# Attention and mixer on one core: q and k of the last three batches turned by transposing transfers instead of TensorE

## The chip, the cores and the metric

The kernel runs on one core of one Trainium2 chip. The metric is the device time of one execution in microseconds; the median of three runs is given. One more execution was taken with the hardware profiler, and its times are those of the views below.

## What is computed

The reference has two parts, one behind the other. The first is a causal attention with a selective bias, for 8 batches of 8 heads with 576 positions of 64 numbers:

```
scores = q @ k^T / 8
cum    = cumsum(max(s, 0))
scores = scores + min(-(cum_i - cum_j), 0), -1e9 above the diagonal
x      = softmax(scores) @ v           # heads side by side: 8 x 576 x 512
```

The second mixes along the sequence by a rank of 32 and then along the channels:

```
u   = x + (x^T U V)^T
out = u + max(u @ w_ch1, 0) @ w_ch2    # 512 -> 2048 -> 512
```

Inputs and output are float32; the kernel works in bf16 with sums in float32.

## The kernel before, in words

**Pairs.** Two heads make a pair, so that there are 32 pairs, n = 0 to 31, four in a batch. The score matmuls (`scores`, L391) need q and k with the 64 numbers of a head on the partitions and the positions along the free axis. Such an operand lies in a slot: 128 partitions x (2 heads) x (576 of q, 576 of k, and a zeroed end). Partitions 64 to 67 hold four rows, pieces of the cumulated s and ones, which add the bias inside the same matmul. From pair 8 on three slots are used in turn (`slot_of`).

**Loads.** GpSimd (POOL) issues the loads of q and k from HBM, float32 turned to bf16 on the way: one transfer for q and one for k of a whole batch, 576 KB each (`load_qk`, L113 for the later batches, L118 for the first). 72 rows lie on the partitions, with 8 runs of 64 numbers for each head. There are two buffers each for q and k, so that the load of batch b waits until the transposes of batch b-2 are over. v goes into one of two slots, by five transfers per batch (L169).

**Turning.** `transposes(n)` turns a pair on TensorE (PE): for each of the two heads four 72x128 blocks of q and four of k, each block a matmul with an identity (L303), into one PSUM tile per head. Two copies per head (64x576, L323) bring it from PSUM into the slot; most are on VectorE (DVE), a few on ScalarE (ACT), by a list in `copies`. Before them the SP queue issues two transfers (L289) that bring the four rows of the pair from a scratch tensor in HBM, `rows_hbm`, which was written once at the start (L222).

**Scores and values.** `scores(n)` makes the scores of a pair in four steps; ACT takes the exponential of each (L409, L421, L427) into pT, and VectorE masks the diagonal blocks (L335). `values(n)` multiplies with v (L455); VectorE makes a reciprocal of the sum (L464) and the quotient x_sb (L465). SP then issues a transposing transfer of x_sb into xT (L472), which the mixing along the sequence (`seqmix`, with uT written at L509) adds later.

**Channel mixing as fill.** `chanmix` makes the hidden layer (L624, evacuated by ACT at L1001) and the output by a scheme with seven products of quarters (L682, sums on VectorE at L660 and L696, stores by SP at L706). It is a generator, and `step_fill` takes one step of it between the steps of attention, so that PE always has work that waits for nothing. At its fourth step a transposing transfer by SP makes u_sd from uT (L988, 128x2048). The PSUM tiles of fill, transposes, values and mixing come in turn from one pool of four buffers (`pwork`).

**Order.** The main loop from L1204 goes over n. In iteration n it makes `transposes(n+1)` with the fill between, then `scores(n)`, then mixing if it is due, then `values(n-1)`. The order on PE and POOL is that of the program. VectorE, ACT and SP also work strictly in order, but for the part after the first batch their order is chosen by a scheduler when the kernel is built.

Of the kernel before, what the change touches and what calls it, by code (L numbers as in the profile page):

```python
# [13 lines left out]
BF16 = mybir.dt.bfloat16  # L14
# [25 lines left out]
def kernel(  # L40
# [12 lines left out]
    nc = tc.nc  # L53
    traced = len(nc.cur_bb.bb.instructions)
    E = mybir.EngineType
    B, H, S, D = q.shape
# [6 lines left out]
    BH = B * H  # L63
    NP = BH // 2
    PB = NP // B
    TP, TT = 72, 8
    NG = B * S // 512
    KA = D + 4
    NF = FF // 128
    FT = 2  # L70

    consts = ctx.enter_context(tc.tile_pool(name="consts", bufs=1))
    loads = ctx.enter_context(tc.tile_pool(name="loads", bufs=2))
# [17 lines left out]
    rows = s_early[:BH, : 8 * S].rearrange("p (r c s) -> p r c s", r=4, c=2)  # L91
# [9 lines left out]
    q_t, k_t = {}, {}  # L101

    def alloc_qk(b):
        q_t[b] = loads.tile([TP, H, TT * D], BF16, tag="q_sd", name="q_sd")
        k_t[b] = loads.tile([TP, H, TT * D], BF16, tag="k_sd", name="k_sd")

    def in_runs(b, h):
        return b > 2 or b == 2 and h >= 4

    def load_qk(b, h, n):  # L110
        for dst, src in ((q_t[b], q), (k_t[b], k)):
# [71 lines left out]
    def slot_of(n):  # L183
        return slots[n % NSLOT if n < 2 * PB else (n + 1) % 3]
# [32 lines left out]
                in_=rows[2 * n + hh : 2 * n + hh + 1].rearrange("n r c s -> n r (c s)"),  # L217
            )

    rows_hbm = nc.dram_tensor("rows_hbm", (4, BH, S), BF16, kind="Internal").ap()  # L220
    for r, n_r, c in ((0, 3, 1), (3, 1, 0)):
        nc.sync.dma_start(  # L222
            out=rows_hbm[ds(r, n_r), ds(2 * PB, BH - 2 * PB)].rearrange("r n s -> n r s"),
            in_=rows[2 * PB :, ds(r, n_r), c, :],
        )

    w1_sb = consts.tile([128, 4, FF], BF16)
    w2_sb = consts.tile([128, NF, DM], BF16)
# [55 lines left out]
    def transposes(n):  # L284
        b, hp = divmod(n, PB)
        slot = slot_of(n)
        if b > 0:
            for r, n_r, c in ((0, 3, 1), (3, 1, 0)):
                nc.sync.dma_start(  # L289
                    out=slot[ds(D + r, n_r), :, ds(c * S, S)],  # L290
                    in_=rows_hbm[ds(r, n_r), ds(2 * n, 2)],
                )
        tps = {}

        def turn(hh, c):
            if c == 0:
                tile = pwork()
                tps[hh] = tile.bitcast(BF16)[:, : 2 * 4 * TP].rearrange(
                    "p (c t m) -> p c t m", c=2, t=4
                )  # L300
            src = (q_t[b], k_t[b])[c]
            for t2 in range(4):
                nc.tensor.transpose(  # L303
                    tps[hh][:, c, t2, :],
                    src[:, 2 * hp + hh, ds(t2 * 128, 128)],
                    identity[:TP, :TP],
                )

        if b == 0:
            for hh in range(2):  # L310
                turn(hh, 0)
            yield
        for hh in range(2):
            if b > 0:
                turn(hh, 0)
            turn(hh, 1)
            tp = tps[hh]
            dst = slot[0:D, hh, 0 : 2 * S]
            for par in range(2):
                src = tp[par * D : par * D + D]  # L320
                if in_runs(b, 2 * hp):
                    by_run = dst.rearrange("p (c t two m) -> p c t two m", c=2, t=4, two=2)
                    copies(n, hh, par)(by_run[:, :, :, par, :], src)  # L323
                else:
                    in_turn = dst.rearrange("p (c m t two) -> p c m t two", c=2, t=4, two=2)
                    copies(n, hh, par)(  # L326
                        in_turn[:, :, :, :, par], src.rearrange("p c t m -> p c m t")
                    )
            yield

    def mask(dst, n_tiles, w, on_pool=False):
        if on_pool:
# [146 lines left out]
    def seqmix(b):  # L479
        x_sb = x_of.pop(b)  # L480
        up = pwork()[:, 0:128]
        for dt in range(4):
            for t in range(5):
                nc.tensor.matmul(
                    up[:, ds(dt * R, R)],
                    lhsT=x_sb[:, dt, t, :],
                    rhs=U_sb[:, t, 0:R],
                    start=(t == 0),
                    stop=(t == 4),
                    skip_group_check=True,  # L490
                )
        uxT = work.tile([128, 128], BF16, tag="uxT", name="uxT")
        nc.vector.tensor_copy(uxT, up)
        yield

        up = pwork()[:, 0:128]
        nc.tensor.matmul(up, lhsT=uxT, rhs=identity, start=True, stop=True)
        ux = work.tile([128, 128], BF16, tag="ux", name="ux")
        nc.vector.tensor_copy(ux, up)
        yield  # L500
        xT = xT_of.pop(b, None)
        cut = 512 - 64 * b

        def evac(dt, lo, hi, src):

            g, at = (b, 64 * b + lo) if lo < cut else (b + 1, lo - cut)
            dst = uT(g)[:, dt, at : at + hi - lo]
            if xT is not None:
                nc.vector.tensor_tensor(dst, src, xT[:, dt, lo:hi], op=ALU.add)  # L509
            elif dt == 2:  # L510
                nc.scalar.copy(dst, src)
            else:
                nc.vector.tensor_copy(dst, src)

        pair = pscore()
        banks = [pair[:, 0:512], pair[:, 512:1024], pwork(), pwork()]
        if xT is None:
            for dt in range(4):
                for t in range(4):
                    nc.tensor.matmul(  # L520
                        banks[dt][:, ds(t * 128, 128)],
                        lhsT=x_sb[:, dt, t, :],
                        rhs=identity,
                        start=(t == 0),
                        stop=False,
                        skip_group_check=True,
                    )
        for dt in range(4):
            nc.tensor.matmul(
                banks[dt],  # L530
                lhsT=ux[ds(dt * R, R), :],
                rhs=V_sb[ds(dt * R, R), 0:512],
                start=(xT is not None),
                stop=True,
                skip_group_check=True,
            )
        pair = pair.rearrange("p (a b) -> p a b", a=2)
        for dt, src in ((slice(0, 2), pair), (2, banks[2]), (3, banks[3])):
            for lo, hi in ((0, cut), (cut, 512)):
                if lo < hi:  # L540
                    evac(dt, lo, hi, src[..., lo:hi])
            yield
        ut = pwork()[:, 0:256].rearrange("p (a b) -> p a b", a=4)
        for dt in range(4):
            if xT is None:
                nc.tensor.matmul(
                    ut[:, dt, :],
                    lhsT=x_sb[:, dt, 4, :],
                    rhs=identity[:, :64],
                    start=True,  # L550
                    stop=False,
                    skip_group_check=True,
                )
            nc.tensor.matmul(
                ut[:, dt, :],
                lhsT=ux,
                rhs=V_end[:, dt, :],
                start=(xT is not None),
                stop=True,
                skip_group_check=True,  # L560
            )
        evac(slice(0, 4), 512, S, ut)
        yield
# [597 lines left out]
    def load(b):  # L1161
        alloc_qk(b)
        for h in range(0, H, 4 if b == 2 else H):
            load_qk(b, h, 4 if b == 2 else H)
# [38 lines left out]
    pace[1] = 11  # L1203
    for n in range(2 * PB, NP + 2):  # L1204
        b, hp = divmod(n, PB)
        if hp == 0 and b < B - 1:
            load(b + 1)
        mixing = seqmix(b - 1) if hp == 1 and b > FT else iter(())
        if b == B:
            fill_with(3)  # L1210
            for _ in range(3):
                step(mixing)
                fill_with(2)
        if n > 2 * PB and n + 1 < NP:
            for at, _ in enumerate(transposes(n + 1)):
                step_fill()
                if at == 0:
                    step(mixing)
        if 2 * PB + 1 < n < NP:
            for at, _ in enumerate(scores(n, pT_of(n))):  # L1220
                step_fill()
                if at == 1:
                    step(mixing)
        for _ in mixing:
            fill_with(1)
        if hp == 1 and FT < b < B:
            fill.append(chanmix(b - 1))
            pace[1] = 12 if b < 6 else 10
        if 2 * PB < n <= NP:
            run(values(n - 1, pT_of(n - 1)))  # L1230
        if hp == 0 and 2 <= b < B - 1:
            load_v(b + 1)
# [70 lines left out]
```

## Time and profile before

| | |
|---|---|
| median of 3 runs | 361.6 us (361.57 to 361.84) |
| the profiled execution | 362.13 us |
| its span, first to last instruction | 360.4 us |
| granted TensorE clock, mean | 0.999 |
| ScalarE busy, VectorE busy | 212.8 us, 274.5 us |
| pairs 20 to 31, transposes on PE | from 161.2 to 262.7 us |
| loads of q of batches 5, 6, 7 issued at | 118.08, 154.91, 192.45 us |
| x_sb into xT, time in SP's queue | 1.2 to 2.1 us, x24 |
| u_sd, time in SP's queue | 1.94 to 8.11 us, x6 |

A timeline has a line for a stretch of equal instructions: start, time, engine, source line, output and inputs, and how many; brackets at the end give the idle time before it and who released it. Durations of matmuls overlap, since they are pipelined; what one costs is seen from the start of the next. "SPq" is the queue of SP: the time that it took to issue a transfer, not the transfer itself. Times of day are microseconds from the start of the span.

### The profile page before, as it was taken

The page shows a single profiled execution, that of the slowest core. Times are in us where ns is not written, and L with a number is a line of the kernel's source. Part 1 is how long each engine was busy: PE and PEld are TensorE (multiplying, and loading weights), DVE is VectorE, ACT ScalarE, POOL GpSimd, SP SyncE. Part 2 cuts the span into 40 slices and gives each one's busy share as a digit, 9 for nine tenths or more (in the row PEclk, how much of TensorE's full clock was granted, in tenths as well). Part 3 has the DMA queues.
Part 4 walks back from the last instruction along what each step waited for, and adds up shares of the span by engine and source line. Part 5 has one row for each costly group of instructions (what it writes and reads, how often), then busy time and mean ns, then how long its engine had stood idle before and what let it go on. Part 6 is the DMA issues. An engine that isn't in the chain of part 4 may idle for free.

```text
span 360.4 us, 9583 instructions
## 1 busy us (share of the span) xinstructions
PE 349.2 (97%) x3987; PEld 256.5 (71%) x4026; DVE 274.5 (76%) x608; ACT 212.8 (59%) x322; POOL 84.1 (23%) x102
## 2 busy tenths in 40 slices
PE   8999999999999999999999999999899999999996
PEld 3685656666598667876688667876488548888885
DVE  8685776688789758985699569985797769676774
ACT  4786966747761677257833786358743554675710
POOL 8897363514040404040304022000000000000000
PEclk9999999999999999999999999999999999999999
DMA  7999999999999999989994999162032515010022
GB/s 101 155 200 196 175 181 102 155 135 136 109 103 106 141 121 81 85 113 123 122 97 66 135 142 85 51 149 58 0 49 67 136 33 116 29 60 31 30 89 87
DMA packets 156163, 37.41 MB, mean 104 GB/s; under 512 B 140760, under 2 KB 154488, under 8 KB 156120
## 3 DMA queue, kind: packets, MB, share of 16 engines
q0 software_dynamic: 113136, 18.50, 90.2%
q1 hardware_dynamic: 42696, 18.11, 29.2%
q8 instruction: 31, 0.51, 0.7%
q10 hardware_dynamic: 288, 0.20, 0.2%
q14 instruction: 12, 0.10, 0.1%
HBM read 37.25 MB, written 9.70 MB: 130 GB/s over the span
## 4 chain that ended last, share of the span: by engine, by line
PE 78%; DVE 8%; ACT 4%; issue 3%; POOL 3%; DMA 2%; DVEq 0%; ACTq 0%; POOLq 0%
PE pwork L624 22%; PE pwork L682 13%; PE quarter L682 10%; PE pscore L391 9%; PE pwork L455 7%; PE parts L912 6%; PE pwork L303 3%; PE pwork L643 3%; DVE uT L509 3%; DMA v_slot<-in_v_dram 2%; ACT pT L409 2%; ACT hT L1001 2%; DVE slot L660 1%; PE pwork L912 1%; PE pscore L624 1%
## 5 line engine op out<-in xcount | busy, mean ns | idle before, releaser
L624 PE MATMUL pwork<-uT,w_sb 128*128 128x512 bf16 x401 | 105.9, 379 | 2.6 <-ACT hT L1001 0.9
L1001 ACT ACTIVATE hT<-pwork 128x512 bf16<-128x512 f32 x108 | 65.2, 608 | 38.4 <-PE pwork L624 38.2
L409 ACT ACTIVATE pT<-pscore 128x1024 bf16<-128x1024 f32 x56 | 56.4, 1030 | 49.0 <-PE pscore L391 48.2
L624 PEld LDWEIGHTS <-w_sb 128*128 128x128 bf16 x448 | 38.3, 98 | 35.9 <-issue 1.3
L391 PE MATMUL pscore<-slot 68*128 68x320 bf16 (+1 forms) x500 | 55.4, 246 | 0.5 <-ACT pT L409 0.2
L391 PEld LDWEIGHTS <-slot 68*128 68x128 bf16 x564 | 41.3, 97 | 16.6 <-issue 1.0
L169 POOL DMA_DIRECT2D v_slot<-in_v_dram x40 | 33.8, 862 | 80.3 <-PE pwork L455 67.7
L682 PEld LDWEIGHTS <-hT 128*128 128x128 bf16 x496 | 46.3, 98 | 7.1 <-DVE uT L509 0.5
L335 DVE TENSOR_TENSOR pT<-pT,keep 128x512 bf16<-128x512 bf16 (+1 forms) x81 | 28.7, 354 | 21.7 <-ACT pT L409 15.9
L323 DVE COPY slot<-pwork 64x576 bf16<-64x576 bf16 x76 | 34.4, 453 | 4.6 <-PE pwork L303 3.7
L455 PEld LDWEIGHTS <-pT 128*128 128x128 bf16 x870 | 32.6, 98 | 7.1 <-issue 1.2
L455 PE MATMUL pwork<-v_slot,pT 128*128 128x65 bf16 x870 | 36.1, 194 | 1.1 <-DVE slot L326 0.6
L465 DVE TENSOR_TENSOR x_sb<-pwork,rec 128x320 bf16<-128x320 f32 x64 | 31.2, 489 | 1.4
L421 ACT ACTIVATE pT<-pscore 128x1024 bf16<-128x1024 f32 x29 | 30.3, 1044 | 2.6 <-PE pscore L391 2.4
L682 PE MATMUL pwork<-w_sb,hT 128*128 128x256 bf16 x240 | 30.6, 273 | 0.0
L326 DVE COPY slot<-pwork 64x576 bf16<-64x576 bf16 x30 | 24.1, 803 | 6.9 <-PE pwork L303 6.5
L682 PEld LDWEIGHTS <-slot 128*128 128x128 bf16 x256 | 24.1, 98 | 4.6 <-issue 1.6
L113 POOL DMA_DIRECT2D q_sd<-in_q_dram x6 | 12.6, 2107 | 44.1 <-PE pwork L303 33.5
L464 DVE RECIPROCAL rec<-pwork 128x5 f32<-128x5 f32 x64 | 12.1, 190 | 13.2 <-PE pwork L455 12.8
L682 PE MATMUL pwork<-w_sum,slot 128*128 128x256 bf16 x160 | 20.3, 272 | 0.7 <-DVE o_sb L696 0.7
L303 PEld LDWEIGHTS <-q_sd 72*128 72x128 bf16 x256 | 14.6, 98 | 8.7 <-DMA q_sd<-in_q_dram 1.1
L303 PE MATMUL pwork<-identity,q_sd 72*128 72x72 bf16 x256 | 18.0, 196 | 0.4 <-DMA q_sd<-in_q_dram 0.4
(164 smaller groups left out, 537.8 us busy)
## 6 DMA issues: line engine op xcount, KB each, us to landing
out_dram<-o_sb SPq DMA_DIRECT2D x34, 256.0 KB
v_slot<-in_v_dram POOLq DMA_DIRECT2D x32, 128.0 KB, 7.2
w_sb<-in_moe_w_ch_dram POOLq DMA_DIRECT2D x4, 1024.0 KB, 13.1
q_sd<-in_q_dram POOLq DMA_DIRECT2D x5, 576.0 KB, 15.1
k_sd<-in_k_dram POOLq DMA_DIRECT2D x5, 576.0 KB, 20.7
q_sd<-in_q_dram POOLq DMA_DIRECT2D x4, 288.0 KB, 13.3
k_sd<-in_k_dram POOLq DMA_DIRECT2D x4, 288.0 KB, 12.1
q_sd<-in_q_dram POOLq DMA_DIRECT2D x4, 144.0 KB, 5.2
```

Source lines behind the costliest of these rows:

```text
L169: nc.gpsimd.dma_start(out=vt[:rows_t, t, :, 0:D], in_=v[b, :, ds(t * 128, rows_t), :].rearrange("h p d -> p h d"),)
L303: nc.tensor.transpose(tps[hh][:, c, t2, :], src[:, 2 * hp + hh, ds(t2 * 128, 128)], identity[:TP, :TP],)
L323: copies(n, hh, par)(by_run[:, :, :, par, :], src)
L335: nc.vector.tensor_tensor(dst, dst, keep[:, :, 0:w].to_broadcast([128, n_tiles, w]), op=ALU.min)
L391: nc.tensor.matmul(dst, lhsT=slot[0:KA, hh, ds(S + j * 128, 128)], rhs=slot[0:KA, hh, lo:hi], start=True, stop=True,)
L409: nc.scalar.activation(pT[:, hh, 0:1024], near, EXP, scale=scale)
L421: nc.scalar.activation(pT[:, :, 1024:1536], mid.rearrange("p (a b) -> p a b", a=2), EXP, scale=scale)
L455: nc.tensor.matmul(po[:, i, :], lhsT=pT[:, hh, ds(place(j, i), 128)], rhs=vt[:, j, h, :], start=(j == 0), stop=(j == i), skip_group_check= ...
L465: nc.vector.tensor_tensor(x_sb[:, hp, :, ds(hh * D, D)], po[:, :, 0:D], rec.to_broadcast([128, 5, D]), op=ALU.mult,)
L624: nc.tensor.matmul(f1, lhsT=w1_sb[:, kt, ds(nf * 128, 128)], rhs=u[:, kt, :], start=(kt == 0), stop=(kt == 3),)
L682: nc.tensor.matmul(acc[:, i, :], lhsT=a[:, kt, ds(i * 128, 128)], rhs=b[:, kt, :], start=(begin and i == 0 and kt == 0), stop=(kt == HF - ...
L1001: nc.scalar.activation(hT[:, nf, :], f1, RELU)
```

## The change

For batches 5, 6 and 7 (`ZB = 5`, pairs 20 to 31) q and k are not turned by PE any more.

- The load puts 96 rows on the partitions, six runs per head, and the two heads of a pair side by side. So it is one transfer per head for q and one for k, sixteen per batch of 144 KB each. They stand in the program at the last pair of batch b-2 rather than at the first of b-1.
- `turn_pair(n+2)`, at the head of iteration n, issues two transposing transfers on SP, one for q and one for k: 96x768 becomes six blocks of 128x96. Head 0 lands on partitions 0 to 63 of the slot, head 1 on 64 to 127, both in the first half of the slot.
- `part_pair(n+1)`, in the place of `transposes(n+1)`, has one VectorE copy, 64x1152, that brings head 1 to partitions 0 to 63 of the second half, and then one transfer of the four rows. These rows lie on partitions 64 to 67, where head 1 lay, so that the transfer waits for the copy.
- The rows of these batches come from a second scratch tensor, `full_hbm`, with the ones already in it, by one transfer instead of two.

```diff
-        q_t[b] = loads.tile([TP, H, TT * D], BF16, tag="q_sd", name="q_sd")
-        k_t[b] = loads.tile([TP, H, TT * D], BF16, tag="k_sd", name="k_sd")
+        rows = TP if b < ZB else TR          # TR, RT = 96, 6
+        q_t[b] = loads.tile([rows, H, TT * D], BF16, tag="q_sd", name="q_sd")
+        k_t[b] = loads.tile([rows, H, TT * D], BF16, tag="k_sd", name="k_sd")
...
+    def by_pairs(tile):
+        return tile.rearrange("p a b -> p (a b)")[:, : PB * RT * 128].rearrange(
+            "p (hp t two d) -> p hp t two d", hp=PB, t=RT, two=2
+        )
+
+    def load_pairs(b):
+        for h in range(H):
+            for dst, src in ((q_t[b], q), (k_t[b], k)):
+                nc.gpsimd.dma_start(
+                    out=by_pairs(dst)[:, h // 2, :, h % 2, :],
+                    in_=src[b, h].rearrange("(t p) d -> p t d", p=TR),
+                )
...
+    full_hbm = nc.dram_tensor("full_hbm", (BH - ZB * H, 4, 2 * S), BF16, kind="Internal").ap()
+    nc.sync.dma_start(
+        out=full_hbm.rearrange("n r s -> n (r s)"),
+        in_=rows[ZB * H :].rearrange("n r c s -> n (r c s)"),
+    )
...
+    def turn_pair(n):
+        b, hp = divmod(n, PB)
+        slot = slot_of(n)
+        for c, src in enumerate((q_t[b], k_t[b])):
+            nc.sync.dma_start_transpose(
+                out=slot[:, 0, ds(c * S, S)].rearrange("p (t m) -> p t m", t=RT),
+                in_=by_pairs(src)[:, hp].rearrange("p t two d -> p (t two d)"),
+            )
+
+    def part_pair(n):
+        slot = slot_of(n)
+        nc.vector.tensor_copy(slot[0:D, 1, 0 : 2 * S], slot[D:, 0, 0 : 2 * S])
+        yield
+        nc.sync.dma_start(
+            out=slot[D:KA, :, 0 : 2 * S],
+            in_=full_hbm[ds(2 * n - ZB * H, 2)].rearrange("h r s -> r h s"),
+        )
+        yield
...
     for n in range(2 * PB, NP + 2):
         b, hp = divmod(n, PB)
-        if hp == 0 and b < B - 1:
+        if hp == 0 and b + 1 < ZB:
             load(b + 1)
+        if hp == PB - 1 and ZB <= b + 2 < B:
+            alloc_qk(b + 2)
+            load_pairs(b + 2)
+        if ZB * PB <= n + 2 < NP:
+            turn_pair(n + 2)
...
-            for at, _ in enumerate(transposes(n + 1)):
+            for at, _ in enumerate((transposes if n + 1 < ZB * PB else part_pair)(n + 1)):
```

## The prediction

> **What bounds the kernel now.** I read the page first, then the clock, then who PE waited for, and then the timelines of PE, VectorE and the DMA queue of SP around the pairs that change.
>
> ```profile
> span 360.4 us, 9583 instructions
> PE 349.2 (97%) x3987; PEld 256.5 (71%) x4026; DVE 274.5 (76%) x608; ACT 212.8 (59%) x322; POOL 84.1 (23%) x102
> ...
> PE 78%; DVE 8%; ACT 4%; issue 3%; POOL 3%; DMA 2%; DVEq 0%; ACTq 0%; POOLq 0%
> ```
>
> PE is busy 97% of the span, 78% of the chain that ended last is PE, and the clock granted is 0.999: time taken off PE's own list comes off the end, if nothing makes PE wait instead. From 140 to 275 us, where the changed pairs run, PE waited for others some 1.6 us in all (0.9 for ACT, 0.7 for VectorE); its list is written out by hand and has a fill matmul beside nearly every step of attention.
>
> The list of PE, 166 to 171 us (start, duration, line, output and inputs, count):
>
> ```profile
> 166.57 0.61 PE L455 MATMUL pwork<-v_slot,pT 128*128 128x65 bf16 x15
> 167.02 1.02 PE L624 MATMUL pwork<-uT,w_sb 128*128 128x512 bf16 x3
> 167.88 0.62 PE L455 MATMUL pwork<-v_slot,pT 128*128 128x65 bf16 x15
> 168.34 1.03 PE L624 MATMUL pwork<-uT,w_sb 128*128 128x512 bf16 x4
> 169.20 0.29 PE L303 MATMUL pwork<-identity,q_sd 72*128 72x72 bf16 x4
> 169.34 0.29 PE L303 MATMUL pwork<-identity,k_sd 72*128 72x72 bf16 x4
> 169.46 1.03 PE L624 MATMUL pwork<-uT,w_sb 128*128 128x512 bf16 x4
> ```
>
> Eight transposes begin at 169.20 and the next fill at 169.46: 0.26 us for eight, although each is recorded as 195 ns long. So a pair's sixteen cost 0.52 us of PE, not 3.1.
>
> **What goes.** (1) 12 pairs x 16 transposes: 12 x 0.52 = 6.3 us of PE, all on the path. The instruction order of the changed kernel has 192 transposes less, and PE's list is otherwise the same, row for row, so that this part happens as described. (2) Four copies per pair from PSUM (0.454 us on VectorE, 0.634 on ACT). Three of the pairs, 22, 26 and 30, have two of theirs on ACT. That is 42 x 0.454 = 19.1 us of VectorE and 6 x 0.634 = 3.8 us of ACT. Both lie beside PE and count only where PE waited: 0.30 and 0.41 us for VectorE (187 and 227 us) and 0.92 us for ACT (256 us, just after 1.27 us of copies of pair 30). I take 1.2 of these 1.6 us. (3) One of two row transfers per pair; it was hidden.
>
> **What comes.** (4) One VectorE copy of 64x1152 bf16 inside SBUF per pair. The nearest rows are the copies of V_sb, 32x576, 301 ns, and of V_end, 32x64, 174 ns, both from partition to partition: by their slope (127 ns per 512 elements) 0.44 us; twice the first, 0.60, is the upper end. 12 x 0.44 = 5.3 us, so VectorE keeps 13.8 us of the 19.1. (5) q and k loaded by sixteen transfers of 144 KB per batch instead of two of 576 KB. The 144 KB loads of the start take 0.72 us of POOL each, the v loads of 128 KB 0.86: some 12.5 us of POOL instead of 4.5. POOL then sits idle 11 us before each such load, waiting for PE (L303), so this costs nothing itself. (6) Two transposing transfers per pair on SP, 96x768 each. The nearest row is the transfer of x_sb, 128x640: 1.2 to 2.1 us of SP's queue, five blocks of 128 columns against six here. I take 1.3 each, 2.6 per pair. (7) The order of waits: transposing transfer, then the copy, then the row transfer, which must wait for the copy because head 1 first lies on the same partitions.
>
> **The new wait.** In the order of the changed kernel the copy of pair m stands on VectorE directly behind x_sb of pair m-4, ahead of the masks of pair m-2, and the transposing transfers wait for the scores of pair m-3, some 2.6 us before that x_sb. With 2.6 us of issue and 1.1 us more until the data is there (the x_sb transfer issued at 154.16 for 1.27 us has its last packet at 156.5), VectorE stands about 1.1 us per pair. Behind the copy are masks that in the light stretches are not due for 3 us, so it is hidden there. In the dense stretches (184 to 198, 216 to 241 us) VectorE is late anyway, and the copies removed stood in the same place. For all these I take 0.7 us, between 0 and 3.
>
> One pair is different: 21. Between the transfers of pairs 20 and 21, SP has to issue two output stores and u_sd. In the profile SP does that here:
>
> ```profile
> 157.26 0.38 SPq L706 DMA_DIRECT2D out_dram<-o_sb  x1
> 158.20 6.89 SPq L988 DMA_TRANSPOSE u_sd<-uT  x1
> 165.14 1.77 SPq L706 DMA_DIRECT2D out_dram<-o_sb  x1
> 167.00 1.01 SPq L289 DMA_DIRECT2D slot<-rows_hbm  x2
> 168.10 1.33 SPq L472 DMA_TRANSPOSE xT<-x_sb  x1
> ```
>
> The same u_sd takes 2.01 us at 239.10, when no loads run, and 6.89 here, beside the loads of batch 6 (POOL issues them at 154.91). Also the x_sb transfer issued at 168.10 has its packets only from 172.5 to 176.2. Pair 21's transfers are behind this u_sd, and VectorE reaches its copy at 161.25:
>
> ```profile
> 160.76 0.49 DVE L465 TENSOR_TENSOR x_sb<-pwork,rec 128x320 bf16<-128x320 f32 x1
> 161.66 0.92 DVE L323 COPY slot<-pwork 64x576 bf16<-64x576 bf16 x2 [0.40 <-PE pwork L303]
> ```
>
> Behind the copy stand the masks of pair 19 (2 x 0.42, 0.22), and reciprocal and x_sb of pair 18 (0.20, 0.49), which alone release a PSUM buffer. The fill at 169.46 takes that buffer again (four buffers in turn, and its weight load waits for VectorE); without the 24 transposes ahead it would start at 168.7. From the arrival T of the data VectorE needs 0.44 + 0.42 + 0.42 + 0.20 + 0.22 + 0.49 = 2.2 us, 1.9 as such rows overlap. So PE waits from T = 166.8 on, and 1 us for each us later. T: u_sd from 158.2 for 2.0 to 6.9 us, I take 4.5, since sixteen small loads leave gaps that two big ones did not; a store, 0.6 (0.38 to 1.77); two issues, 2.6; and from there to the landing 1.1 to some 6.7 us (the 168.10 transfer: 176.2 less 169.4), I take 3.5. Sum 169.4, **a wait of 2.6 us**; from both ends, 0 (T = 164.3) to 9.3 (176.1, with 1.77 for the store 177.3: 10.5).
>
> The second u_sd under load, 8.11 us at 197.08, should escape: batch 7's loads no longer wait for the transposes of pair 23 on PE (191.99) but for its transfers, some 10 us earlier, and are over by about 198.
>
> **The skill, weighed.** The 128 KB v loads are issued 0.85 us apart (five in 4.23 us) and land 7.2 us after issue, so they overlap. The Trainium skill, DMA: Bandwidth & Descriptors, section Bandwidth, advises transfers of 1 MiB or more, and gives about 2.0 us plus bytes/436e3 per GpSimd transfer; sixteen in series would by an estimate from it take 37 us per batch, as long as a batch lasts, against 6.7 before, and the end would come later by several us. The row speaks against the series. For the transposing transfers, the x_sb one moves 164 KB in 1.1 us of packets. The same page (Latency and other measured facts) has 261 GB/s, by which a pair's 295 KB would take 1.1 us instead of 2.0, and T would be 0.9 us earlier.
>
> **Sum.** -6.3 (PE) -1.2 (waits that end with the copies) +2.6 (pair 21) +0.7 (other pairs) = -4.2 us. The profiled execution took 362.1 us, a span of 360.4 with 1.7 around it, so it would be 357.9; the median of the runs is 361.6, 0.5 less, which makes **357.4 us**.
>
> **Rivals.** A: loads in small pieces let u_sd through, T stays under 166.8. For it: 2.0 us in the quiet; against it: the loads begin at 156 and last past 165. -6.3 -1.2 +0.3 = -7.2: 354.4 us. B: the engines go on giving the loads the upper hand, T near 176, a wait of 9.3 us, and the chain of transfer, copy, row, next transfer catches up only over the following pairs, so that the dense work of VectorE after 174 us (sums of hidden, uT) starts late: 2 us more. -6.3 -0.5 +9.3 +2 = +4.5: **366 us, slower**. It decides as soon as T passes 166.8 + 7.5 = 174.3. For it: the 176.2 above. C: the same wait at 5 to 7.5 us: the gain is used up, 360 to 362 us. That the transposes don't go is excluded by the order.
>
> **Chances.** Forecast (355.5 to 360) 0.40; A 0.30; C 0.10, half of it within 0.2% (0.7 us, about what a measurement of this kernel can tell from no change); B 0.20. So faster 0.75, same 0.05, slower 0.20. The range goes from 354.0 (A with all of the 1.6 us) to 363.0, which leaves out most of B.
>
> **What would show it.** PE loses 192 matmuls and about 6 us of busy time; VectorE ends near 261 us busy, ACT near 209. If the step on pair 21 is right, VectorE idles some 8 us before its copy at 161 us with a DMA as releaser, and PE has its longest idle time near 169 us, released by VectorE; with A there is none, with B it is over 8 us. The u_sd near 197 us should take about 2 us of SP. The prediction fails if copies stand long at other pairs, or if the transposing transfers of 96 rows take much longer than those of 128.

## The result, and the profile after

The changed kernel takes **365.77 us** (median of 4 runs, 365.32 to 365.84) beside 361.72 for the kernel before on the same chip: a ratio of 1.0108, 95% interval 1.0091 to 1.0126. It is 4.0 us slower where 4.2 us less were forecast; 365.8 lies above the range given (354.0 to 363.0) and beside rival B (366). The profiled execution took 365.84 us.

The same lines of the page as before, with the row of PE and of its clock from the forty slices:

```profile
span 364.1 us, 9312 instructions
...
PE 347.3 (95%) x3834; PEld 250.5 (69%) x3834; DVE 260.5 (72%) x578; ACT 209.1 (57%) x316; POOL 105.7 (29%) x144
...
PE   8999999999999999996798999999999999999996
PEclk9999999999999999999899999999999999999999
...
PE 73%; DMA 11%; DVE 9%; ACT 3%; issue 2%; SPq 1%; POOL 0%; DVEq 0%; ACTq 0%; POOLq 0%
...
L363 DVE COPY slot<-slot 64x1152 bf16<-64x1152 bf16 x12 | 5.6, 468 | 33.9 <-DMA slot<-k_sd 33.9
...
q_sd<-in_q_dram POOLq DMA_DIRECT2D x24, 72.0 KB, 6.3
```

PE lost its transposes, VectorE ended at 260.5 us busy and ACT at 209.1, but DMA rose from 2% of the chain to 11%. PE has one hole, in slices 19 and 20 (some 164 to 182 us), and in the second of them the clock falls. The group of the new copies shows where DMA comes in: VectorE stood 33.9 us in all ahead of ten of the twelve copies, released each time by the transposing transfer of k. The last line (the count holds the loads of q alone; k has as many) gives the size of a small load: 72 KB for one head, not the 144 KB that the account of the change and the prediction have.

VectorE around the hole (start, duration, line, output and inputs; in brackets the idle time before it and who ended it):

```profile
161.77 0.49 DVE L505 TENSOR_TENSOR x_sb<-pwork,rec 128x320 bf16<-128x320 f32 x1
173.24 0.46 DVE L363 COPY slot<-slot 64x1152 bf16<-64x1152 bf16 x1 [10.98 <-DMA slot<-k_sd]
173.72 0.76 DVE L375 TENSOR_TENSOR pT<-pT,keep 128x512 bf16<-128x512 bf16 x2
...
174.62 0.49 DVE L505 TENSOR_TENSOR x_sb<-pwork,rec 128x320 bf16<-128x320 f32 x1
```

PE there, to be laid beside its list of before:

```profile
168.36 0.62 PE L495 MATMUL pwork<-v_slot,pT 128*128 128x65 bf16 x15
168.81 1.03 PE L664 MATMUL pwork<-uT,w_sb 128*128 128x512 bf16 x4
175.17 1.89 PE L664 MATMUL pwork<-uT,w_sb 128*128 128x512 bf16 x4 [5.33 <-DVE x_sb L505]
```

The copy of pair 21 waits 11 us for its data. The masks of pair 19 and the x_sb of pair 18 stand behind it, although everything that they need is there. The x_sb at 174.62 frees the PSUM buffer that the fill wants, and PE starts again at 175.17. The chain is the one that the prediction drew; the four fill matmuls then take 1.89 us instead of 1.03. The reason is in the stretches of 2 us (length, then busy time of PE, PEld, DVE, ACT and POOL, the granted clock, DMA, GB/s):

```profile
172.00:174.00 2.00, 0.00 (x0) 0.00 (x0) 0.73 (x2) 0.00 (x0) 0.00 (x0) 1.00 2.27 154
174.00:176.00 2.00, 0.83 (x3) 0.28 (x3) 1.70 (x7) 0.00 (x0) 0.00 (x0) 0.72 0.84 83
176.00:178.00 2.00, 2.00 (x10) 1.07 (x9) 0.00 (x0) 0.65 (x2) 0.00 (x0) 0.50 1.06 98
178.00:180.00 2.00, 2.00 (x14) 1.02 (x13) 0.75 (x2) 1.90 (x3) 0.00 (x0) 0.92 0.47 89
```

Around its restart PE was granted half its clock for 3.4 us (174.89 to 178.30). Its next three groups take 1.68, 0.87 and 1.15 us from start to start, where the same three take 0.87, 0.44 and 0.87 us at the full clock: 1.5 us more.

Why the data came so late, from the queue of SP:

```profile
159.20 3.88 SPq L1028 DMA_TRANSPOSE u_sd<-uT  x1
163.18 0.56 SPq L746 DMA_DIRECT2D out_dram<-o_sb  x1
163.91 1.36 SPq L356 DMA_TRANSPOSE slot<-q_sd  x1
165.35 1.40 SPq L356 DMA_TRANSPOSE slot<-k_sd  x1
166.85 2.06 SPq L512 DMA_TRANSPOSE xT<-x_sb  x1
```

The transfers of pair 21 are issued by 166.75, and their copy can begin only at 173.24. POOL issues the sixteen loads of batch 6 from 155.87 to 169.2 us.

Where the time came and went, as the start of a pair's last score matmuls minus that of before (us; the last four columns are experiments told below):

| pair | after | e4 | e5 | e9 | e10 |
|---|---|---|---|---|---|
| 17 | 0.0 | -0.3 | -0.5 | +0.1 | -0.3 |
| 18 | +1.1 | +0.8 | +0.4 | +1.2 | +0.7 |
| 20 | +7.0 | -0.3 | -0.8 | +0.1 | -0.4 |
| 22 | +6.9 | -0.9 | +3.0 | +2.8 | -1.9 |
| 26 | +5.0 | -2.8 | +2.5 | +0.9 | -3.9 |
| 30 | +4.0 | -3.2 | +2.1 | -1.3 | -6.0 |

The transposes of a pair stood ahead of the scores of the pair before it, so that the twelve steps from pair 18 to pair 30 should bring 0.52 us each. The changed kernel loses 1.1 us at pair 18 and 7.0 at pair 20 (5.5 until PE starts again, at 175.17 where the fill was due at 169.7, and 1.5 of clock). It loses 1.1 at pair 22 (the copy of pair 24 waits 3.7 us and PE idles 1.3), and from pair 26 to 30 it gains 1.0 of the 2.1 due. -6.3 + 1.1 + 7.0 + 1.1 + 1.1 = +4.0.

### The profile page after: what moved, and what is told of

Its sections match the earlier page's. It is cut to its first block, busy times and chain, and to the rows that moved or that the text cites. A ratio compares the mean times of both kernels' runs of the same rounds, so it can differ in the third digit from the quotient of the medians.

```text
span 364.1 us, 9312 instructions
## 1 busy us (share of the span) xinstructions
PE 347.3 (95%) x3834; PEld 250.5 (69%) x3834; DVE 260.5 (72%) x578; ACT 209.1 (57%) x316; POOL 105.7 (29%) x144
## 4 chain that ended last, share of the span: by engine, by line
PE 73%; DMA 11%; DVE 9%; ACT 3%; issue 2%; SPq 1%; POOL 0%; DVEq 0%; ACTq 0%; POOLq 0%
PE pwork L664 21%; PE quarter L722 10%; PE pwork L722 10%; PE pscore L431 8%; PE pwork L495 6%; DMA slot<-k_sd 6%; PE parts L952 6%; DMA xT<-x_sb 4%; PE pwork L683 3%; PE pwork L324 2%; DVE slot L347 2%; DVE uT L549 1%; DVE o_sb L736 1%; PE pscore L392 1%; ACT hT L1041 1%
## 5 line engine op out<-in xcount | busy, mean ns | idle before, releaser
L664 PE MATMUL pwork<-uT,w_sb 128*128 128x512 bf16 x432 | 108.1, 382 | 6.5 <-DVE x_sb L505 5.5
L375 DVE TENSOR_TENSOR pT<-pT,keep 128x512 bf16<-128x512 bf16 (+1 forms) x81 | 28.2, 352 | 13.3 <-ACT pT L449 7.8
L363 DVE COPY slot<-slot 64x1152 bf16<-64x1152 bf16 x12 | 5.6, 468 | 33.9 <-DMA slot<-k_sd 33.9
L347 DVE COPY slot<-pwork 64x576 bf16<-64x576 bf16 x30 | 24.1, 802 | 6.7 <-PE pwork L324 6.3
L121 POOL DMA_DIRECT2D q_sd<-in_q_dram x24 | 17.8, 743 | 27.5 <-PE pwork L324 23.5
L722 PE MATMUL quarter<-w_sb,hT 128*128 128x256 bf16 x144 | 18.0, 273 | 0.3 <-DVE uT L549 0.3
L121 POOL DMA_DIRECT2D k_sd<-in_k_dram x24 | 17.7, 738 | 1.3 <-DMA k_sd<-in_k_dram 1.2
## 6 DMA issues: line engine op xcount, KB each, us to landing
q_sd<-in_q_dram POOLq DMA_DIRECT2D x4, 288.0 KB, 13.3
```

What stands on the lines that cost most here:

```text
L121: nc.gpsimd.dma_start(out=by_pairs(dst)[:, h // 2, :, h % 2, :], in_=src[b, h].rearrange("(t p) d -> p t d", p=TR),)
L347: copies(n, hh, par)(in_turn[:, :, :, :, par], src.rearrange("p c t m -> p c m t"))
L375: nc.vector.tensor_tensor(dst, dst, keep[:, :, 0:w].to_broadcast([128, n_tiles, w]), op=ALU.min)
L664: nc.tensor.matmul(f1, lhsT=w1_sb[:, kt, ds(nf * 128, 128)], rhs=u[:, kt, :], start=(kt == 0), stop=(kt == 3),)
L722: nc.tensor.matmul(acc[:, i, :], lhsT=a[:, kt, ds(i * 128, 128)], rhs=b[:, kt, :], start=(begin and i == 0 and kt == 0), stop=(kt == HF - ...
```

## The experiments

The theory after this reading: PE's gain is real, and it is lost because VectorE reaches copies whose transfers are late, with other work queued behind them. Three things could make them late: u_sd ahead of them in SP's queue, the active loads of batch 6, and the place of the copy in VectorE's order. The rivals: many small loads cost by themselves; transfers are too slow for the scores whatever the order. Each ratio is to the kernel before, run on the same chip.

| run | median us | ratio | 95% interval |
|---|---|---|---|
| e1 | 366.61 | 1.0132 | 1.0107 to 1.0157 |
| e2 | 372.57 | 1.0304 | 1.0253 to 1.0354 |
| e3 | 362.16 | 1.0004 | 0.9996 to 1.0013 |
| e4 | 358.88 | 0.9919 | 0.9904 to 0.9934 |
| e5 | 366.09 | 1.0115 | 1.0100 to 1.0129 |
| e6 | 359.00 | 0.9924 | 0.9905 to 0.9942 |
| e7 | 361.09 | 0.9987 | 0.9971 to 1.0003 |
| e8 | 363.65 | 1.0055 | 1.0032 to 1.0078 |
| e9 | 360.57 | 0.9960 | 0.9935 to 0.9986 |
| e10 | 356.03 | 0.9839 | 0.9826 to 0.9851 |
| e11 | 356.61 | 0.9853 | 0.9820 to 0.9887 |
| e12 | 353.46 | 0.9780 | 0.9767 to 0.9794 |

**e1: one copy later.** `placed` ties a VectorE instruction behind the one that the program wrote before it.

```diff
-        nc.vector.tensor_copy(slot[0:D, 1, 0 : 2 * S], slot[D:, 0, 0 : 2 * S])
+        (placed if n == 21 else lambda f: f())(lambda: nc.vector.tensor_copy(
+            slot[0:D, 1, 0 : 2 * S], slot[D:, 0, 0 : 2 * S]))
```

> One edit of the changed kernel: VectorE's copy for pair 21 stands behind the masks of pair 19 and the two x_sb of pair 18 instead of ahead of them; its row transfer goes out one transposing pair later on SP. The transfers themselves stay as late as they were (copy at about 173). Theory (VectorE's order hands the late transfers to TensorE): the 5.3 us of PE idle before 175.2 shrinks to under 2, the granted clock stays at 1.00 there, and the time is 358 to 361 us. Rival 1 (the transfers are late for the scores of pair 21 too, whatever stands behind the copy): PE waits as long, at the scores, and the time stays at 364 to 366. Rival 2 (transfers and loads slow PE or VectorE all along, the one wait is a symptom): no change, 365 to 366.

The time, 366.61, is near both rivals', but neither's mechanism came. PE's hole at 170 us is gone (pair 20 is 0.4 ahead of before). Now the copy of pair 22, next on VectorE, waits until 177.30 with the masks of pair 20 and the x_sb of pair 19 behind it, and PE idles 3.9 us at 177.8 and 1.9 at 188.7, each with 3.4 us of half clock after it. The wait moved by one copy.

**e2: u_sd out of the way.**

```diff
-            if g > 0 and nf == 3:
-                u_sd = by_token(u)
+            if g > 0 and nf == 12:
+                (u_sd issued behind the SP transfer that the program wrote last)
```

> The changed kernel with one group of SP's issues moved: in batches 3 to 7 the large transposing transfer u_sd is issued behind the q and k transfers, the xT transfer and the row transfer of the next pair instead of ahead of them. Orders of PE, VectorE, ACT and POOL stay. Theory (the pair's transfers queue behind u_sd): the transfers of pair 21 are issued near 160 instead of 163.9, VectorE's copy comes at 164 to 167 instead of 173.2, PE's idle there falls from 5.3 to under 1, no clock dip, and the time is 356.5 to 359.5 us. Rival (the loads of batch 6 alone make them late, u_sd is innocent): the copy still comes at 170 or later, the time is 362 or more.

Both failed. The transfers of pair 21 were issued at 161.2 instead of 163.9 and the copy came at 169.42, between the two numbers: 5.4 us after the last issue, almost as long as with u_sd ahead. PE's idle time there did fall from 5.3 to 0.84 us, as the theory had it. And u_sd, now between the row of pair 21 and the transfers of pair 22, held those until 173.87; the copy of pair 22 waited 6.7 us, PE 3.6 us behind it, and 3.5 us more at 235.5 for an o_sb whose u_sd was late. Moving u_sd brought the copy of pair 21 forward by 3.8 us, about half of what leaving out the loads brings (7.3 us, e4), and handed the wait to the next pair.

**e3: small loads alone**, in the kernel before.

```diff
-        for h in range(0, H, 4 if b == 2 else H):
-            load_qk(b, h, 4 if b == 2 else H)
+        n = 4 if b == 2 else 1 if b > 4 else H
+        for h in range(0, H, n):
+            load_qk(b, h, n)
```

> The kernel before, with the two q and k loads of each of batches 5 to 7 cut into sixteen of one head each, as many as the change issues; nothing is turned by transfers. Theory (the number of loads costs nothing by itself, POOL has time): 361.7 us, within 0.7. Rival (POOL's or the DMA engines' work for many small loads costs several us by itself): 363.5 or more.

362.16 beside 362.01: no cost. The loads hurt only where something waits for transfers that run beside them. The run also shows what small loads do to u_sd, here beside sixteen of them:

```profile
158.25 3.81 SPq L988 DMA_TRANSPOSE u_sd<-uT  x1
```

Beside two large loads it took 6.89 us (the kernel before); the next u_sd under load, at 197 us, takes 4.70 here and 8.11 there. So the prediction's ground for 4.5 us, and for rival A, was sound: small loads do let u_sd through sooner.

**e4: no loads of batch 6.**

```diff
+            if b + 2 == 6:
+                q_t[6], k_t[6] = q_t[5], k_t[5]
+            else:
-            alloc_qk(b + 2)
-            load_pairs(b + 2)
+                alloc_qk(b + 2)
+                load_pairs(b + 2)
```

> The changed kernel without the sixteen loads of batch 6: its q and k are not loaded, its pairs are worked out from those of batch 5, so that the work and every order but POOL's stay; the loads of batch 7 stay. Theory (u_sd and the active loads each slow the transfers of pair 21): u_sd's issue takes about 2 instead of 3.9 us, the landing after the last issue about 2.5 instead of 6.5, VectorE's copy comes at 166 to 168 instead of 173.2, PE's idle is under 0.5, no clock dip, and the time is 357 to 359.5 us. Rival (u_sd's place in the queue alone makes them late, the loads cost nothing): the copy comes at 171 or later and the time is 362 or more.

SP's queue in this run:

```profile
158.90 1.93 SPq L1028 DMA_TRANSPOSE u_sd<-uT  x1
160.92 0.95 SPq L746 DMA_DIRECT2D out_dram<-o_sb  x1
162.04 1.23 SPq L356 DMA_TRANSPOSE slot<-q_sd  x1
163.37 1.22 SPq L356 DMA_TRANSPOSE slot<-k_sd  x1
```

and the copy of pair 21 on VectorE:

```profile
165.95 0.46 DVE L363 COPY slot<-slot 64x1152 bf16<-64x1152 bf16 x1 [4.00 <-DMA slot<-k_sd]
```

The theory held, and the landing was quicker still than it said (about 2.5 us). Without the loads u_sd takes 1.93 us instead of 3.88, and the copy starts 1.4 us after the last issue instead of 6.5. PE has neither a hole nor a dip of the clock there. By the trace's packet records the 2048 packets of u_sd, 256 bytes each, go out at 473 to 846 in each microsecond here and at 192 to 573 in the changed kernel, where the 128-byte packets of the loads run between them. That the same kernel is 3.1 us faster than before (358.88 beside 362.01) shows that the loss at pair 21 decides the sign.

**e5: the same loads, spread.** Four loads behind each transposed pair, into the place that it has left.

```diff
-        if hp == PB - 1 and ZB <= b + 2 < B:
+        if hp == PB - 1 and b + 2 == ZB:
             alloc_qk(b + 2)
             load_pairs(b + 2)
         if ZB * PB <= n + 2 < NP:
             turn_pair(n + 2)
+            later, at = divmod(n + 2 + PB, PB)
+            if later < B:
+                q_t[later], k_t[later] = q_t[ZB], k_t[ZB]
+                load_pairs(later, (2 * at, 2 * at + 1))
```

> The changed kernel with the same q and k loads at other times: batches 6 and 7 are loaded pair by pair, four loads behind each transposed pair into the place that this pair has left, instead of sixteen in one burst. Everything else, the orders of PE, VectorE, ACT and SP among it, stays. Theory (the burst of batch 6's loads is what makes the transfers of pair 21 late): VectorE's copy for pair 21 comes at 165 to 167 instead of 173.2, PE's 5.3 us of idle and the clock dip there are gone, and the time is 357.5 to 360 us. Rival (the loads slow the transfers by the same total wherever they lie, the wait only moves to other pairs): 362 us or more.

The copies of pairs 21 and 22 on VectorE:

```profile
165.81 0.46 DVE L363 COPY slot<-slot 64x1152 bf16<-64x1152 bf16 x1 [4.28 <-DMA slot<-k_sd]
174.06 0.46 DVE L363 COPY slot<-slot 64x1152 bf16<-64x1152 bf16 x1 [5.04 <-DMA slot<-k_sd]
```

The first line is the theory's, the time the rival's: 366.09. Pair 21 is on time, but the four loads that follow it (165.05 to 169.0) run beside the transfers of pair 22 (issued 166.79 to 169.32), whose copy waits 5.0 us; PE then loses 1.0 us for x_sb and 1.9 for ux (the mixing along the sequence), with half a clock after it. This was the fastest of its runs, 363.95, so the median holds some 2 us that no trace shows.

**e6: spread loads and later copies.** e5 with the edit of e1 for all pairs above 20 (`n > 20`).

> As e5_spread_loads, and VectorE's copies from pair 21 on stand in the order in which the program writes them, behind the x_sb of the pair three before instead of four before; their row transfers move behind the next pair's transfers on SP. Theory (what is left of the loss after e5 is copies that VectorE reaches before their transfers have landed): VectorE's idle ahead of the copies falls from about 27 us to under 15, PE's waits for x_sb and o_sb between 185 and 250 fall from about 3 us to under 1.5, and the time is 1 to 2 us below e5, 356 to 358.5. Rival (the row transfers, now later, keep the scores waiting): the same as e5 or slower, 359 or more.

359.00 is just above the theory's 358.5, but 7.1 us below e5, where the rival saw no gain on it: the theory. No copy above pair 20 waits any more. One wait is left that the kernel before did not have, on PE:

```profile
PE pscore L431 <- DMA slot<-full_hbm: 2.2, 1, 2.2
```

It is the row transfer of pair 24, which now stands behind u_sd, a store and xT: its copy is over at 197.33, it is issued at 201.84, and it lands at 207.

**e7: the last batch alone.** `ZB = 7` instead of 5.

> The change for the last batch only (pairs 28 to 31); its sixteen loads lie in a stretch without transposed pairs. 64 transposes leave PE, 2.1 us. Theory (in the changed kernel pairs 28 to 31 gained nothing, because copies that wait for transfers hold x_sb, o_sb and uT there): 361 to 362.3 us, no gain beside 361.7. Rival (every pair whose loads are out of the way gains its 0.52 us): 359.3 to 360.3.

361.09 beside 361.80. The number is the theory's; the interval, 0.9971 to 1.0003, does not exclude a small gain, and in its trace the last batch brings 1.0 us of its 2.1. The copy of pair 30 waits 4.3 us and that of pair 31 2.3, with no load active. So part of the loss needs no loads at all.

**e8: four batches with spread loads.** e5 with `ZB = 4`.

> As e5_spread_loads, with four batches (pairs 16 to 31) turned by transfers instead of three; 64 more transposes leave PE, 2.1 us. Theory (0.5 us a pair is gained where the copy finds its transfers landed): 1 to 2.5 us below e5, 355.5 to 358.5. Rival (each further pair adds as much wait as it saves): within 0.7 us of e5.

363.65, 2.4 us below e5, though both are far above the numbers given, which rested on e5's. Its runs lie between 361.4 and 366.1, so it decides little. PE idles 1.93, 1.92 and 2.51 us in its trace, and the clock stays at 1.00 (more on this at the end).

**e9: later copies, loads in a burst.** The edit of e6 on VectorE alone.

> The changed kernel with its burst of loads, and VectorE's copies from pair 21 on in the order in which the program writes them (as in e6_spread_and_later_copies, without its spread loads). The transfers of pair 21 still land near 173. Theory A (VectorE's order is the main loss, the loads only make it show): copies no longer hold masks or x_sb, PE waits at most 2 to 3 us in all for rows of pairs 21 and 24, and the time is 359 to 361 us, near e6. Theory B (late transfers are a loss by themselves, through the scores): PE waits 4 us or more at the scores of pair 21, with the clock dip behind it, and the time is 363 us or more.

360.57 (358.06 to 362.24): theory A. The copies of pairs 21 and 22 on VectorE, and PE's longest idle time:

```profile
173.36 0.46 DVE L363 COPY slot<-slot 64x1152 bf16<-64x1152 bf16 x1 [3.50 <-DMA slot<-k_sd]
178.24 0.57 DVE L363 COPY slot<-slot 64x1152 bf16<-64x1152 bf16 x1 [2.30 <-DMA slot<-k_sd]
...
180.20 0.54 PE L524 MATMUL pwork<-U_sb,x_sb 128*128 128x32 bf16 x15 [1.88 <-DVE x_sb L505]
```

The copy of pair 21 still starts at 173.36, and PE has no hole at 170 us. The order of eleven copies, and of the rows behind them, is worth 5.2 us of the kernel's time (365.77 less 360.57) with the transfers of pair 21 as late as before. What is left is at the copy of pair 22, reached at 176 us and fed at 178.24: PE idles 1.9 us, again with a dip of the clock. So theory B's part is smaller but there. From pair 26 to pair 30 the kernel now gains 2.1 us, all that is due (+0.9 to -1.3), with the loads where they were: what took it away in the changed kernel was the place of the copies.

**e10: rows by ACT.** e6, with the row transfers on ACT's queue.

```diff
-        nc.sync.dma_start(
+        nc.scalar.dma_start(
             out=slot[D:KA, :, 0 : 2 * S],
```

> As e6_spread_and_later_copies, with the row transfers issued by ACT instead of SP. Theory (what is left there is the row of pair 24, 2.2 us of PE idle, landing 5 us after its issue because it stands behind u_sd and xT in SP's queue): this wait goes, the clock dip with it, and the time is 1.5 to 3.5 us below e6, 355.5 to 357.5. Rival (ACT, waiting for each copy ahead of its row, holds exps and hidden activations): the same as e6 or slower, 359 or more.

```profile
span 354.1 us, 9320 instructions
...
PE 345.3 (98%) x3834; PEld 250.1 (71%) x3834; DVE 262.2 (74%) x578; ACT 209.0 (59%) x316; POOL 105.5 (30%) x144
...
PE 80%; DVE 9%; ACT 4%; DMA 4%; issue 2%; SPq 0%; POOL 0%; DVEq 0%; ACTq 0%; POOLq 0%
```

356.03: the theory. This page reads as the prediction wanted it: PE 98%, DMA down to 4% of the chain, no hole. The row of pair 24 goes out at 197.70, as its copy ends. From pair 18 to pair 30 the kernel gains 6.7 us on before. ACT, whose queue issues the row in 0.25 to 0.5 us, loses nothing that shows.

**e11 and e12: four batches**, e6 and e10 with `ZB = 4` and later copies from pair 17 on.

> As e6_spread_and_later_copies for four batches (pairs 16 to 31). 64 more transposes leave PE, 2.1 us. Theory (with loads spread and copies late a pair's 0.52 us is gained in full): 1.5 to 2.5 us below e6, 356 to 357.5. Rival (rows and transfers behind each further u_sd wait as much as is saved): within 0.7 us of e6, or slower.

> As e10_rows_on_act_queue (loads spread, copies later, rows issued by ACT) for four batches, pairs 16 to 31. 64 more transposes leave PE, 2.1 us. Theory (with its three waits mended, turning a pair by transfers is worth its 0.52 us of PE): 1.5 to 2.5 us below e10, 353.5 to 354.5. Rival (the four further pairs meet waits of their own, as e11 did, which was 2.4 below e6 with wide scatter): 355 to 356.5.

e11 is 2.4 us below e6, with wide scatter (354.1 to 358.5). e12 takes 353.46 us, 2.57 below e10 and 2.2% below the kernel before: four more pairs at 0.5 us and a little more. In its trace, between 140 and 275 us, PE has no idle time above 0.2 us but one of 0.93 for ACT, which the kernel before has too. It is the best version found.

## Why the prediction was wrong, step by step

- **PE's transposes, -6.3 us: right.** Each step that meets no wait gains 0.51 to 0.54 us (e9, to pairs 23, 24 and 28 to 30), and e10 gains 6.7 over the twelve.
- **Waits that end with the copies, -1.2 us: wrong.** Of 0.30 (187 us), 0.41 (227) and 0.92 us (256) on PE, the changed kernel still has 0.41 and 0.69; the 0.30 is gone, and one of 0.31 for an o_sb at 245 us has come. In e10 those for VectorE are gone, but ACT's is there with 0.93: it was not caused by the copies that went.
- **The wait at pair 21, +2.6 us: the failing step.** The mechanism was right to the instruction: the copy waits for a DMA, masks and x_sb stand behind it, PE stops at the fill after 168.81. The sum of T was 169.4 and came out at 173.24: u_sd starts 1.0 later, takes 0.6 less, store and gaps 0.2 more, the issues 0.2 more, and **the landing 6.5 us instead of 3.5**. The row of 6.7 us stood in the prediction as the upper end; e4 shows that the loads of batch 6 make 5.1 of the 6.5. PE's idle time was 5.3 us. By the prediction's rule it would have been 6.4 (173.24 less 166.8), but the fill that waits was due at 169.7, a microsecond later than the 168.7 drawn, so that 5.5 us were lost where 2.6 were put. The step of rival B, a delay caught up only slowly, was not needed.
- **What was missing: the clock.** Half a clock for 3.4 us, which cost 1.5 us, is in no term, though a wait of 2.6 us might have drawn it too: in e6 one of 2.2 did, in e8 one of 2.5 did not.
- **Other pairs, +0.7 us: too small.** They cost 3.3, just above the bound of 3: 1.1 at pair 18 (the copy of pair 20 delays the x_sb behind it, PE idles 0.9), 1.1 at pair 22, and 1.1 of the last batch's gain. The prediction saw that a copy stands on VectorE about 1.1 us early per pair and took it as hidden; ten copies waited 33.9 us, and e9 shows that it was not hidden.
- **The terms together.** 2.9 us more at pair 21 until PE starts again, 1.5 of clock, 2.6 more at other pairs and 1.2 of waits that did not end make the 8.2 us between -4.2 and +4.0.
- **Rival B's point of decision** was T = 174.3. The kernel was slower already at 173.24, because the clock and the other pairs took what was left of the gain.
- **Predicted and seen:** VectorE and ACT busy as forecast, the copy 0.46 us (0.44), an issue 1.20 us for q and 1.22 for k in the median, the longest 2.30 (1.3), POOL 0.74 us for each small load, 11.8 for sixteen (some 12.5), the second u_sd in 1.92 us at 207 (about 2). PE has 192 weight loads fewer, but its busy time fell by 1.9 us, not by about 6; in e10, with no dip of the clock, it fell by 3.9. VectorE's idle time before the copy was 11 us, not 8. The small loads did not run in series: batch 6's were issued within 13.3 us, and in the median they landed 6.3 (q) and 6.6 us (k) after issue.
- **Open:** which resource the loads share with the transposing transfers; the runs show only that packets of both interleave and both slow down. Rows on ACT's queue without the other two edits were not tried, so the three have no separate prices in every order. The clock's cost was not taken away by itself. The traced execution of the changed kernel had a mean clock of 0.995, the three others 0.990, and all four took 365.3 to 365.8 us: the split between waiting and clock given here is that of one execution.

## What to carry to other kernels

A copy that waits for a transfer should stand in its engine's order where the data is surely there, behind all work that is ready: here that alone was worth 5.2 us, and the scheduler's order had put it too early. Time a transfer on the critical path beside the loads that will run with it, not by its quiet row, and give small late transfers a queue of their own. Reckon that a PE idle stretch of 2 us may cost nearly twice as much: half a clock for 3.4 us can add up to 1.7, and whether it comes is not settled by the length of the stretch alone.

## What the runs showed of the hardware

**The clock.** PE's granted clock fell to 0.50 for 3.41 us after idle stretches of 1.9 (e1, e2, e5, e9), 2.2 (e6), 3.5 and 3.6 (e2), 3.9 (e1) and 5.3 us (after), and stayed at 1.00 after those of 1.4 us (e2) and less. But three stretches of e8, of 1.9, 1.9 and 2.5 us, drew no dip at all. The longest, with the granted clock behind it (third number from the end):

```profile
223.10 0.39 PE L569 MATMUL pscore<-V_sb,ux 32*128 32x512 bf16 x2 [2.51 <-DVE ux L539]
...
223.00:227.00 4.00, 3.49 (x35) 2.87 (x36) 3.96 (x11) 0.58 (x1) 1.58 (x3) 1.00 2.36 140
```

After 5.3 us the dip was there when PE began again; after 1.9 us it came 0.7 (e5), 1.2 (e2), 1.4 (e1) and 2.4 us (e9) after PE was back at work. Dips of one run begin whole numbers of 3.413 us apart: at 181.82 and 192.06 in e1 (3 times), at 184.21, 194.45 and 238.82 in e2 (3 and 13 times). In the 3.41 us ahead of each dip PE was busy between 0 (after) and 1.86 us (e9). The Trainium skill (TensorE: Matmul & The Clock Gate, sections What's actually happening and Why this matters for your kernels) has a free-running window of 3413 ns, half the clock after an idle one, and the advice to leave no idle gap above some 3 us. The depth and the length of the dips and their distances agree with these runs; the gap that was enough here is shorter than the advice says, and the window ahead of a dip was not wholly idle. The place of a gap in such windows may be why 1.9 us drew a dip and 2.5 us did not; no run moves a gap alone to show it, and no bound comes out of the busy time either, since a window with 1.78 us of work in the changed kernel (from 168.06) was followed by none.

What a dip costs shows in e9's nine executions: the three at a mean clock of 1.000 took 358.1 to 359.7 us, the two at 0.995 took 360.3 and 360.6, and the four at 0.991 took 361.5 to 362.2. One dip lowers the mean by 0.005 (half of 3.41 in 359 us).

**Transfers.** A transposing transfer beside GpSimd's loads took about twice as long to issue (u_sd 3.88 us against 1.93), and 6.5 instead of 1.4 us from the last issue to the copy that waits for it.
